# Decayed block attention feeding a SiLU MLP: transposes of q and k moved from TensorE to the DMA engines, and attention from block 8 on given due times

## The chip, the cores and the metric

One NeuronCore of a Trainium2 chip runs the whole program in one launch. The metric is device time in microseconds (us) of that core; lower is better. Times are medians over runs of the same kernel. One further execution was taken with the hardware profiler, and all durations below come from that execution.

## The reference

The input is q, k, v with 4 batches, 8 heads, 768 positions and 64 channels, a decay `lam` per head, and two weight matrices. The attention works on 64-position blocks with a running state per head:

```
intra = (qb @ kb.T * Dmask) @ vb            # Dmask[i,j] = lam**(i-j) for i >= j, else 0
inter = (qb * lam**(pos+1)) @ kv_state
out   = intra + inter
kv_state = lam**64 * kv_state + (kb * lam**(63-pos)).T @ vb
```

The attention result is laid out as x with 3072 rows (batch and position) and 512 columns (head and channel). Then comes the MLP: `h = x @ w_in` (512 to 2048), `g = h * sigmoid(h)`, `y = g @ w_out` (2048 to 512). The output is y, 3072 x 512 in float32.

## The kernel before

The kernel works on 24 blocks of 128 positions: block `u` belongs to batch `u // 6`, and the six blocks of a batch are chained through the state. Decay is folded into q and k: `qs` is q times a power of lam, `ks` is k times the inverse power, so the mask is only zeros and ones.

For each block the attention does this:

- SyncE (SP) issues the loads of k, v and q (`kf`, `vf`, `qf`). From block 2 to block 21, q comes for two blocks at once. All loads are issued in one fixed order from one queue, SP's, which also issues the output stores.
- VectorE makes `qs` (L315) and `ks` (L369) in bf16. For the first blocks (`u < WIDE`, WIDE = 8) `ks` is written into a zero-padded buffer instead (`kp`, L361), so that one transposed tile holds every head by itself.
- TensorE transposes `qs` (L327, four 128x128 matmuls per block) and `ks` (L389, four; with the padded form L377, eight) into a PSUM bank `tr_ps`. ScalarE, sometimes VectorE, copies the results out of PSUM (helper lines L224 and L226) to `qT` and to the zero-padded `kTz`.
- TensorE forms the scores `st_ps` (L415, eight matmuls), VectorE masks them into `st_sb` (L424), TensorE forms `x_ps` from the scores and from the state (L453, L457), and ScalarE copies that to `xt`, the transposed input of the MLP.
- TensorE forms the state's update `d_ps` (L484; in the padded form L480), VectorE adds it to the state (`y`, L500), and GpSimd scales by the decay (`Xz`, `Xf`, L229).

The MLP is done for groups of blocks. `first_product` (L545) multiplies `xt` of one group with `w_in`, ScalarE applies SiLU into `g` (L554), and `second_product` (L573; the last block L612) multiplies by `w_out`. VectorE copies the result out and SP stores it. A group of four blocks has matmuls with 512 moving columns, a group of two has 256, a group of one has 128.

The order of the work on every engine is fixed when the program is built. The class `Plan` holds every step with the cost that it books for it, its dependences, its ring buffers and a priority. It walks through time, always takes the step that can start first, and writes out the program in that order. The chip then runs each engine's list in order: an instruction that has to wait holds back everything behind it on its engine. `after` on a step adds booked time behind its dependences; a step on the engine `NONE` costs nothing and only delays what depends on it. Loads are written out 1.8 us ahead of the time at which they are booked (`AHEAD`). Where the plan leaves TensorE without work early on, `idle` fills the gap with matmuls on zeros (`warm_ps`, L650), of which it adds as many as fit:

```
us = 0.44 if a < 6 else 0.22
n = int(0.8 * (b - a - 0.2) / us)
if n < 2 or a > 90 or since > a: return
```

Of the kernel before, what the change touches and what calls it, by code (L numbers as in the profile page):

```python
# [8 lines left out]
BF16 = mybir.dt.bfloat16  # L9
# [4 lines left out]
class Plan:  # L14
# [3 lines left out]

    AHEAD = 1.8
    AWAY = 0.6  # L20
    LAT = {"SP": 0.0, "NONE": 0.0, "STORE": 2.0, "PE": 0.25, "DVE": 0.12, "ACT": 0.16, "POOL": 0.15, "DMA": 0.1}

    def __init__(self):
        self.ops = []
        self.rings = {}

    def op(self, engines, deps, fn, prio, alloc=(), frees=(), after=0.0):


        o = dict(engines=engines, deps=[d for d in deps if d is not None], fn=fn, prio=prio,  # L30
                 alloc=list(alloc), frees=list(frees), id=len(self.ops), end=None, slots={}, after=after)
        self.ops.append(o)
        return o

# [12 lines left out]
    def run(self, start, idle=None):  # L47
        INF = float("inf")
        free = dict(start)
        users = {}  # L50
        for o in self.ops:
            o["wait"] = len(o["deps"])
            for d in o["deps"]:
                users.setdefault(d["id"], []).append(o)
        ready = [o for o in self.ops if o["wait"] == 0]
        out = []
        while ready:
            pick = {}
            for o in ready:
                slots = max([self.slot(a)[1] for a in o["alloc"]] or [0.0])  # L60
                if slots == INF:
                    continue
                if "SP" in o["engines"]:
                    slots += self.AHEAD
                at = {e: max([free[e] if e != "NONE" else 0.0, slots] + [o["after"] + d["end"] + (self.LAT[d["eng"]] if d["eng"] != e else 0.0)
                                                 for d in o["deps"]]) for e in o["engines"]}
# [33 lines left out]
def kernel(  # L100
# [20 lines left out]
    KI = DM // 128  # L121
    KO = DFF // 128
    HB = BLK // 2
    WIDE = 8

    ctx.enter_context(tc.manual_schedule())
    const = ctx.enter_context(tc.tile_pool(name="const", bufs=1))
# [1 line left out]
    ps = ctx.enter_context(tc.tile_pool(name="ps", bufs=1, space=bass.MemoryType.PSUM))  # L129

    plan = Plan()
    BUFS = dict(kf=6, vf=6, qf=3, wst=6, qs=2, qT=4, ks=4, g=34, st_sb=6, o_sb=3, y=2, Xf=2,
                kTz=3, vz=3, Xz=2, kp=3)
    for name, n in BUFS.items():
        plan.ring(name, n)
    plan.ring("bank", 8, pick=True)
# [4 lines left out]
    def sb(o, name, shape, dtype, tag=None):  # L141
        return work.tile(shape, dtype, tag=tag or name, bufs=BUFS[tag or name], name=name)

    def bank(o, name, shape, dtype):
# [5 lines left out]
        out=lam_sb,  # L150
        in_=bass.AP(tensor=lam.tensor, offset=lam.offset, ap=[[0, 128]] + list(lam.ap)),
# [17 lines left out]
        out=ident, in_=ident, compare_op=AL.not_equal, fill=1.0,  # L169
# [6 lines left out]
        out=mask, in_=mask, compare_op=AL.is_ge, fill=0.0,  # L176
# [3 lines left out]
    kTz = [const.tile([128, NP, 2, BLK], BF16, name=f"kTz{i}") for i in range(BUFS["kTz"])]  # L180
# [22 lines left out]
    for hh in range(2):  # L203
        r = slice(64 * hh, 64 * hh + 64)
# [6 lines left out]
    w_in_r = moe_w_in.rearrange("(ko p) f -> p ko f", p=128)  # L211
    w_out_r = moe_w_out.rearrange("(ko p) f -> p ko f", p=128)

    groups = [[0, 1], [2, 3], [4], [5], [6, 7]] + [list(range(u, u + 4)) for u in range(8, NU, 4)]
    group_of = {u: (g, i) for g, us in enumerate(groups) for i, u in enumerate(us)}
    xts = [const.tile([128, KI, len(us) * BLK], BF16, name=f"xt{g}") for g, us in enumerate(groups)]

    plain = {0, 1, NU - 2, NU - 1}

    val = {}  # L220

    def copy(o, dst, src):
        if o["eng"] == "ACT":
            nc.scalar.activation(dst, src, AF.Copy)  # L224
        else:
            (nc.vector if o["eng"] == "DVE" else nc.gpsimd).tensor_copy(dst, src)  # L226
# [68 lines left out]
    O = {}  # L295

    def attention(u):
        b, blk = divmod(u, NB)
        pr = at["v", u]


        if u in plain or u % 2 == 0:
            two = u not in plain
            lq = load["q", u]
            late = []
            if u >= 8:
                late = [plan.op({"NONE": 0.0}, [lq], lambda o: None, 0, after=4.0)]
            halves = []
            for t in range(2 if two else 1):
                def fn(o, t=t, first=(t == 0)):  # L310
                    qf = val["qf", u]
                    if first:
                        val["qs", u] = sb(o, "qs", [128, 2, H, 64], BF16)
                    src = qf.rearrange("p h (t d) -> p h t d", t=2)[:, :, t, :] if two else qf
                    nc.vector.tensor_tensor(  # L315
                        val["qs", u][:, t], src,
                        lam_fwd[:, 1 + t if two else 0, :, None].to_broadcast([128, H, 64]), op=AL.mult)
                halves.append(plan.op(
                    {"DVE": 0.7}, [lq] + late + halves[:1], fn, pr + 0.1, alloc=["qs"] if t == 0 else [],
                    frees=[(lq, lq["tag"])] if t == two else []))  # L320
            trs = []
            for t in range(len(halves)):
                def fn(o, t=t):
                    if t == 0:
                        val["trq", u] = bank(o, "tr", [128, len(halves), NP, BLK], BF16)
                    for i in range(NP):
                        nc.tensor.transpose(val["trq", u][:, t, i, :], val["qs", u][:, t, 2 * i:2 * i + 2, :], ident)  # L327
                trs.append(plan.op({"PE": 0.225}, [halves[t]] + trs[:1], fn, pr + 0.1,
                                   alloc=["bank", "n_tr"] if t == 0 else [],
                                   frees=[(halves[0], "qs")] if t == len(halves) - 1 else []))  # L330
            evs = []
            for t in range(len(halves)):
                def fn(o, t=t):
                    if t == 0:
                        val["qT", u] = sb(o, "qT", [128, 2, NP, BLK], BF16)
                    copy(o, val["qT", u][:, t], val["trq", u][:, t])
                evs.append(plan.op({"ACT": 0.6, "DVE": 0.69}, [trs[t]] + evs[:1], fn, pr + 0.1,
                                   alloc=["qT"] if t == 0 else [],
                                   frees=[(trs[0], "bank"), (trs[0], "n_tr")] if t == len(halves) - 1 else []))
            O["qT", u] = evs  # L340
            if two:
                O["qT", u + 1] = evs
        home = u if u in plain else u - u % 2

        def qT(p):
# [5 lines left out]

        lk, lv = load["k", u], load["v", u]
        late = []
        if u >= 8:
            late = [plan.op({"NONE": 0.0}, [lv], lambda o: None, 0, after=4.0)]

        wide = u < WIDE
        if wide:
# [14 lines left out]
        if wide:  # L373
# [9 lines left out]
            kz = [plan.op({"ACT": 1.02, "DVE": 1.22}, [tk], fn, pr, alloc=["kTz"],  # L383
                          frees=[(tk, "bank"), (tk, "n_tr")])]
        else:
            def fn(o):
                val["trk", u] = bank(o, "tr", [128, NP, BLK], BF16)
# [135 lines left out]
        O["vz", u] = (vc, oo, dd)  # L523

    for u in range(NU):
        attention(u)
    for vc, oo, dd in (O["vz", u] for u in range(NU) if ("vz", u) in O):
        done = plan.op({"NONE": 0.0}, [oo, dd], lambda o: None, 0, frees=[(vc, "vz")])

# [120 lines left out]
                nc.tensor.matmul(t, lhsT=zeros[:, 0:128], rhs=zeros, start=True, stop=True)  # L650
        seq.append((a, len(seq), dict(fn=fn)))

    seq = plan.run({"PE": 1.9, "DVE": 4.2, "ACT": 5.9, "POOL": 5.0, "SP": 3.7, "STORE": 0.0, "NONE": 0.0}, idle)
    for _, _, o in seq:
        o["fn"](o)

# [29 lines left out]
```

## Time and profile before

| | us |
|---|---|
| median of 3 runs | 235.52 (235.09 to 236.05) |
| profiled execution, device time | 237.28 |
| its span in the profile | 235.6 |
| TensorE busy in the span | 221.8 |
| VectorE busy | 114.7 |
| ScalarE busy | 121.9 |
| GpSimd busy | 53.1 |

The profiled execution is 1.76 us above the median of the unprofiled runs, and 1.7 us of its device time lie outside the span. The span has three parts. Until about 30 us the first blocks' attention runs with little for TensorE to do beside it. From about 30 to 134 us attention and MLP matmuls are interleaved. From 134 us to the end only MLP matmuls are left. The granted TensorE clock was 0.998 of full speed over the span. TensorE's instructions are pipelined, so the time that one costs is the distance from its start to the next one's start, which is shorter than the duration that the group rows show for one.

### The profile page before, as it was taken

How to read it: one execution, taken by the hardware profiler on the slowest of the kernel's cores; microseconds unless marked ns; L12 is line 12 of the kernel's file. 1: busy time of each engine (PE TensorE's matmuls, PEld its weight loads, DVE VectorE, ACT ScalarE, POOL GpSimd, SP SyncE). 2: the span in 40 equal slices, each digit the busy share in tenths (PEclk: the TensorE clock that was granted, in tenths of full speed). 3: DMA queues.
4: the chain of work that ended last, by engine and by line, in shares of the span. 5: the costliest groups of instructions: out<-in, count | busy, mean ns of one | idle time of the engine just before them, and what ended most of it. 6: DMA issues, size and time to landing. Idle time of an engine off the chain costs nothing.

```text
span 235.6 us, 4440 instructions
## 1 busy us (share of the span) xinstructions
PE 221.8 (94%) x1799; PEld 136.3 (58%) x1799; DVE 114.7 (49%) x184; ACT 121.9 (52%) x213; POOL 53.1 (23%) x71
## 2 busy tenths in 40 slices
PE   4889898999999999979999999999999999999994
PEld 1656687899756676746667544444444444444453
DVE  5677755694359999998997211012100111021221
ACT  5585477867777699869976422401275023710000
POOL 7354420340045244642476100000000000000000
PEclk9999999999999999999999999999999999999999
DMA  6999989999999999999200122204400232023232
GB/s 124 237 288 298 294 227 226 296 363 318 221 228 245 255 262 222 233 238 219 46 1 12 35 47 45 45 2 87 92 0 0 45 75 61 0 45 83 56 86 89
DMA packets 73060, 33.85 MB, mean 144 GB/s; under 512 B 55376, under 2 KB 66000, under 8 KB 73040
## 3 DMA queue, kind: packets, MB, share of 16 engines
q1 hardware_dynamic: 72896, 33.50, 60.4%
q8 instruction: 14, 0.23, 0.4%
q10 hardware_dynamic: 144, 0.07, 0.1%
q14 instruction: 6, 0.05, 0.1%
HBM read 27.27 MB, written 6.29 MB: 142 GB/s over the span
## 4 chain that ended last, share of the span: by engine, by line
PE 52%; DVE 2%; DMA 1%; ACT 1%; issue 0%; DVEq 0%
PE o_ps L573 28%; PE h_ps L545 19%; PE x_ps L453 1%; PE st_ps L415 1%; DVE st_sb L424 1%; PE o_ps L612 1%; DMA out_dram<-o_sb 1%; PE x_ps L457 1%; PE d_ps L484 1%; PE tr_ps L327 0%; PE tr_ps L389 0%; DVE ks L369 0%; DVE y L500 0%; ACT kTz L224 0%; DVE o_sb L226 0%
## 5 line engine op out<-in xcount | busy, mean ns | idle before, releaser
L545 PE MATMUL h_ps<-xt,w_in_bf 128*128 128x512 bf16 (+2 forms) x576 | 88.9, 308 | 0.0
L554 ACT ACTIVATE g<-h_ps 128x512 bf16<-128x512 f32 x96 | 56.3, 597 | 59.2 <-PE h_ps L545 33.0
L573 PE MATMUL o_ps<-w_out_bf,g 128*128 128x512 bf16 x368 | 83.3, 379 | 0.5 <-DVE st_sb L424 0.5
L545 PEld LDWEIGHTS <-w_in_bf 128*128 128x128 bf16 x576 | 49.7, 98 | 29.1 <-DVE w_in_bf L226 0.3
L226 DVE COPY o_sb<-o_ps 128x512 f32<-128x512 f32 (+2 forms) x24 | 15.9, 663 | 87.1 <-PE o_ps L573 84.5
L573 PEld LDWEIGHTS <-g 128*128 128x128 bf16 x368 | 35.2, 98 | 39.6 <-issue 0.7
L229 POOL TENSOR_TENSOR Xz<-y,lam_blk 64x256 bf16<-64x256 f32 x40 | 34.3, 858 | 75.0 <-DVE y L500 46.0
L424 DVE TENSOR_TENSOR st_sb<-st_ps,mask 128x512 bf16<-128x512 f32 x48 | 30.9, 683 | 6.0 <-PE st_ps L415 5.7
L224 ACT ACTIVATE kTz<-tr_ps 64x512 bf16<-64x512 bf16 (+1 forms) x38 | 25.8, 680 | 6.6 <-PE tr_ps L377 2.2
L315 DVE TENSOR_TENSOR qs<-qf,lam_fwd 128x512 bf16<-128x512 f32 x24 | 20.2, 861 | 5.0 <-DMA qf<-in_q_dram 5.0
L224 ACT ACTIVATE xt<-x_ps 128x512 bf16<-128x512 f32 x24 | 14.2, 594 | 9.2 <-PE x_ps L457 8.8
L453 PE MATMUL x_ps<-st_sb,vz 128*128 128x128 bf16 x192 | 18.0, 219 | 0.2
L453 PEld LDWEIGHTS <-vz 128*128 128x128 bf16 x192 | 15.1, 98 | 5.4 <-issue 1.2
L500 DVE TENSOR_TENSOR y<-d_ps,Xf 64x256 f32<-64x256 f32 (+1 forms) x27 | 11.3, 419 | 9.9 <-issue 7.6
L415 PE MATMUL st_ps<-qT,kTz 128*128 128x128 bf16 x192 | 15.1, 222 | 0.5 <-ACT qT L224 0.3
L224 ACT ACTIVATE qT<-tr_ps 128x512 bf16<-128x512 bf16 x22 | 12.8, 594 | 4.4 <-PE tr_ps L327 4.3
L229 POOL TENSOR_TENSOR Xf<-y,lam_blk 128x256 f32<-128x256 f32 x16 | 14.5, 909 | 1.3
L457 PE MATMUL x_ps<-qT,Xz 128*128 128x128 bf16 x80 | 14.5, 219 | 0.0
L415 PEld LDWEIGHTS <-kTz 128*128 128x128 bf16 x192 | 12.5, 99 | 3.1 <-ACT kTz L224 1.0
L224 ACT ACTIVATE o_sb<-o_ps 128x512 f32<-128x512 f32 (+1 forms) x2 | 0.9, 438 | 25.6 <-DMA out_dram<-o_sb 25.6
L369 DVE TENSOR_TENSOR ks<-kf,lam_bwd 128x512 bf16<-128x512 f32 x16 | 14.0, 879 | 0.3
L327 PE MATMUL tr_ps<-ident,qs 128*128 128x128 bf16 x96 | 9.1, 223 | 4.0 <-DVE qs L315 3.8
(54 smaller groups left out, 115.8 us busy)
## 6 DMA issues: line engine op xcount, KB each, us to landing
kf<-in_k_dram SPq DMA_DIRECT2D x24, 256.0 KB, 5.5
vf<-in_v_dram SPq DMA_DIRECT2D x24, 256.0 KB, 5.3
out_dram<-o_sb SPq DMA_DIRECT2D x41, 128.0 KB, 2.4
qf<-in_q_dram SPq DMA_DIRECT2D x10, 512.0 KB, 5.9
wst<-in_moe_w_in_dram SPq DMA_DIRECT2D x8, 512.0 KB, 6.9
wst<-in_moe_w_out_dram SPq DMA_DIRECT2D x8, 512.0 KB, 7.3
qf<-in_q_dram SPq DMA_DIRECT2D x4, 256.0 KB, 5.1
out_dram<-o_sb SPq DMA_DIRECT2D x3, 256.0 KB, 3.6
```

Source lines behind the costliest of these rows:

```text
L224: nc.scalar.activation(dst, src, AF.Copy)
L226: (nc.vector if o["eng"] == "DVE" else nc.gpsimd).tensor_copy(dst, src)
L229: (nc.vector if o["eng"] == "DVE" else nc.gpsimd).tensor_tensor(dst, a, b, op=op)
L315: nc.vector.tensor_tensor(val["qs", u][:, t], src, lam_fwd[:, 1 + t if two else 0, :, None].to_broadcast([128, H, 64]), op=AL.mult)
L369: nc.vector.tensor_tensor(val["ks", u], val["kf", u], lam_bwd[:, :, None].to_broadcast([128, H, 64]), op=AL.mult)
L415: nc.tensor.matmul(val["st", u, half][:, i, :], lhsT=val["kTz", u][:, h // 2, h % 2, :], rhs=qT(h // 2), start=True, stop=True)
L424: nc.vector.tensor_tensor(val["st_sb", u, half], val["st", u, half], m[:, None, :].to_broadcast([128, 4, BLK]), op=AL.mult)
L453: nc.tensor.matmul(x[:, p, :], lhsT=vp[:, p, hh, :], rhs=val["st_sb", u, h // 4][:, h % 4, :], start=(hh == 0), stop=(hh == 1 and blk == 0))
L457: nc.tensor.matmul(x[:, p, :], lhsT=val["Xz", u][:, p, :], rhs=qT(p), start=False, stop=True)
L545: nc.tensor.matmul(t[:, j, :], lhsT=w_in_bf[:, ko, (m * per + j) * 128:(m * per + j + 1) * 128], rhs=xts[g][:, ko, :], start=(ko == 0), st ...
L554: nc.scalar.activation(t, val["h", g, m], AF.Silu)
L573: nc.tensor.matmul(val["o", u], lhsT=val["g", g, ko][:, i * BLK:(i + 1) * BLK], rhs=w_out_bf[:, ko, :], start=(ko == 0), stop=(ko == KO - 1))
```

## The change

- From block 8 on (`XB = 8`) the transposes of `qs` and `ks` are DMA transposes, issued by SP from SBUF to SBUF. The q transpose of a pair of blocks is one DMA of 128 x 1024 bf16, that of a single block and each k transpose one of 128 x 512. The k transposes land in a new ring `kT` (3 buffers), and ScalarE or VectorE copies them from there to `kTz`. `qT` is written by the DMA itself.
- The plan knows these DMAs as an engine of their own, `XBAR`, with 2.0 us booked per 512 columns. What reads the result is booked no earlier than 6.0 us after that.
- Attention steps from block 8 on get due times: `pace(u)` is 57.0 + 5.5 (u - 8) us. Their q, k and v are used no earlier than that, and no earlier than 2.0 us after the load's booked end (4.0 before). For blocks 4 to 7 that delay is 1.2 us (none before). TensorE steps of the attention from block 8 on get `after = 0.8`.
- `WIDE` goes from 8 to 4, so that blocks 4 to 7 use the unpadded form. The ring `qf` has 2 buffers in place of 3.
- Blocks 8 to 11 form two groups of two in place of one group of four.

```diff
+    XB = 8
-    WIDE = 8
+    WIDE = 4
-    BUFS = dict(kf=6, vf=6, qf=3, ...
+    BUFS = dict(kf=6, vf=6, qf=2, ... kT=3)
-    groups = [[0, 1], [2, 3], [4], [5], [6, 7]] + [list(range(u, u + 4)) for u in range(8, NU, 4)]
+    groups = [[0, 1], [2, 3], [4], [5], [6, 7], [8, 9], [10, 11]] + [list(range(u, u + 4)) for u in range(12, NU, 4)]
+    def pace(u):
+        return 0.0 if u < 8 else 57.0 + 5.5 * (u - 8)
...
-            if u >= 8:
-                late = [plan.op({"NONE": 0.0}, [lq], lambda o: None, 0, after=4.0)]
+            if u >= 4:
+                late = [plan.op({"NONE": 0.0}, [lq], lambda o: None, 0, after=2.0 if u >= 8 else 1.2, at=pace(u))]
...
+            if u >= XB:
+                n = len(halves)
+                def fn(o):
+                    val["qT", u] = sb(o, "qT", [128, 2, NP, BLK], BF16)
+                    nc.sync.dma_start_transpose(
+                        out=val["qT", u][:, 0:n].rearrange("p t a s -> p (t a) s"),
+                        in_=val["qs", u][:, 0:n].rearrange("p t h d -> p (t h d)"))
+                x = plan.op({"XBAR": 2.0 * n}, [halves[-1]], fn, pr + 0.1, alloc=["qT"], frees=[(halves[0], "qs")])
+                O["qT", u] = [x, plan.op({"NONE": 0.0}, [x], lambda o: None, 0, after=6.0)]
...
+        elif u >= XB:
+            def fn(o):
+                val["kT", u] = sb(o, "kT", [128, NP, BLK], BF16)
+                nc.sync.dma_start_transpose(
+                    out=val["kT", u], in_=val["ks", u].rearrange("p h d -> p (h d)"))
+            tk = plan.op({"XBAR": 2.0}, [ks], fn, pr, alloc=["kT"])
+            landed = plan.op({"NONE": 0.0}, [tk], lambda o: None, 0, after=6.0)
+            ...
+                    copy(o, val["kTz", u][r, :, hh, :], val["kT", u][r])
+                kz.append(plan.op({"ACT": 0.59, "DVE": 0.35}, [tk, landed] + kz[:1], fn, pr, ...
...
     for u in range(NU):
+        n = len(plan.ops)
         attention(u)
+        if u >= 8:
+            for o in plan.ops[n:]:
+                if "PE" in o["engines"]:
+                    o["after"] = 0.8
```

More of the change, by code (lines that the diff above doesn't have):

```diff
@@ L20 @@
     AWAY = 0.6
-    LAT = {"SP": 0.0, "NONE": 0.0, "STORE": 2.0, "PE": 0.25, "DVE": 0.12, "ACT": 0.16, "POOL": 0.15, "DMA": 0.1}
+    LAT = {"SP": 0.0, "XBAR": 0.0, "NONE": 0.0, "STORE": 2.0, "PE": 0.25, "DVE": 0.12, "ACT": 0.16, "POOL": 0.15, "DMA": 0.1}
     def __init__(self):
@@ L25, in __init__, with op @@
         self.rings = {}
-    def op(self, engines, deps, fn, prio, alloc=(), frees=(), after=0.0):
+    def op(self, engines, deps, fn, prio, alloc=(), frees=(), after=0.0, at=0.0):
         o = dict(engines=engines, deps=[d for d in deps if d is not None], fn=fn, prio=prio,
-                 alloc=list(alloc), frees=list(frees), id=len(self.ops), end=None, slots={}, after=after)
+                 alloc=list(alloc), frees=list(frees), id=len(self.ops), end=None, slots={}, after=after, at=at)
         self.ops.append(o)
@@ L64, in run @@
                     slots += self.AHEAD
-                at = {e: max([free[e] if e != "NONE" else 0.0, slots] + [o["after"] + d["end"] + (self.LAT[d["eng"]] if d["eng"] != e else 0.0)
+                at = {e: max([free[e] if e != "NONE" else 0.0, slots, o["at"]] + [o["after"] + d["end"] + (self.LAT[d["eng"]] if d["eng"] != e else 0.0)
                                                  for d in o["deps"]]) for e in o["engines"]}
@@ L131 @@
     plan = Plan()
-    BUFS = dict(kf=6, vf=6, qf=3, wst=6, qs=2, qT=4, ks=4, g=34, st_sb=6, o_sb=3, y=2, Xf=2,
-                kTz=3, vz=3, Xz=2, kp=3)
+    BUFS = dict(kf=6, vf=6, qf=2, wst=6, qs=2, qT=4, ks=4, g=34, st_sb=6, o_sb=3, y=2, Xf=2,
+                kTz=3, vz=3, Xz=2, kp=3, kT=3)
     for name, n in BUFS.items():
@@ L321, in attention @@
             trs = []
-            for t in range(len(halves)):
+            if u >= XB:
[7 more added lines that the diff above has]
+                O["qT", u] = [x, plan.op({"NONE": 0.0}, [x], lambda o: None, 0, after=6.0)]
+            for t in range(len(halves) if u < XB else 0):
                 def fn(o, t=t):
@@ L331, in attention @@
             evs = []
-            for t in range(len(halves)):
+            for t in range(len(halves) if u < XB else 0):
                 def fn(o, t=t):
@@ L339, in attention @@
                                    frees=[(trs[0], "bank"), (trs[0], "n_tr")] if t == len(halves) - 1 else []))
-            O["qT", u] = evs
+            if u < XB:
+                O["qT", u] = evs
             if two:
-                O["qT", u + 1] = evs
+                O["qT", u + 1] = O["qT", u]
         home = u if u in plain else u - u % 2
@@ L353, in attention @@
         late = []
-        if u >= 8:
-            late = [plan.op({"NONE": 0.0}, [lv], lambda o: None, 0, after=4.0)]
+        if u >= 4:
+            late = [plan.op({"NONE": 0.0}, [lv], lambda o: None, 0, after=2.0 if u >= 8 else 1.2, at=pace(u))]
         wide = u < WIDE
@@ L384, in attention, with fn @@
                           frees=[(tk, "bank"), (tk, "n_tr")])]
+        elif u >= XB:
[5 more added lines that the diff above has]
+            landed = plan.op({"NONE": 0.0}, [tk], lambda o: None, 0, after=6.0)
+            kz = []
+            for hh in range(2):
+                def fn(o, hh=hh):
+                    if hh == 0:
+                        val["kTz", u] = kTz[o["slots"]["kTz"]]
+                    r = slice(64 * hh, 64 * hh + 64)
+                    copy(o, val["kTz", u][r, :, hh, :], val["kT", u][r])
+                kz.append(plan.op({"ACT": 0.59, "DVE": 0.35}, [tk, landed] + kz[:1], fn, pr,
+                                  alloc=["kTz"] if hh == 0 else [], frees=[(tk, "kT")] if hh else []))
         else:
@@ L651, in idle @@
         seq.append((a, len(seq), dict(fn=fn)))
-    seq = plan.run({"PE": 1.9, "DVE": 4.2, "ACT": 5.9, "POOL": 5.0, "SP": 3.7, "STORE": 0.0, "NONE": 0.0}, idle)
+    seq = plan.run({"PE": 1.9, "DVE": 4.2, "ACT": 5.9, "POOL": 5.0, "SP": 3.7, "STORE": 0.0, "NONE": 0.0, "XBAR": 0.0}, idle)
     for _, _, o in seq:
```

## The prediction

> **What bounds the kernel now.** I read the page first, then busy time by stretch, then the chain of waits, then TensorE's and VectorE's instructions in order of time, and last the DMA queue of the loading stretch.
>
> From the page:
>
> ```profile
> span 235.6 us, 4440 instructions
> ...
> PE 221.8 (94%) x1799; PEld 136.3 (58%) x1799; DVE 114.7 (49%) x184; ACT 121.9 (52%) x213; POOL 53.1 (23%) x71
> ...
> PE   4889898999999999979999999999999999999994
> ...
> DVE  5677755694359999998997211012100111021221
> ...
> DMA  6999989999999999999200122204400232023232
> ```
>
> A slice is 5.9 us. TensorE is full from slice 8 to the end but for one dip at about 103 us. VectorE is full only in slices 13 to 21 (71 to 124 us), and the DMA engines are full until slice 19 and nearly idle after it. By stretch (busy us of PE, PEld, DVE, ACT, POOL; clock; DMA share; GB/s):
>
> ```profile
> 30.00:60.00 30.00, 28.24 (x398) 26.42 (x396) 19.91 (x32) 22.26 (x36) 6.51 (x8) 1.00 1.04 283
> 60.00:110.00 50.00, 48.23 (x478) 32.88 (x476) 42.61 (x67) 40.15 (x73) 20.29 (x22) 1.00 1.08 238
> 110.00:130.00 20.00, 19.54 (x201) 13.33 (x200) 16.78 (x29) 15.95 (x30) 11.19 (x14) 1.00 0.23 42
> 130.00:236.00 106.00, 102.25 (x505) 48.30 (x503) 14.46 (x22) 25.70 (x45) 0.18 (x1) 0.99 0.22 49
> ```
>
> From 30 to 130 us TensorE idles 1.76 + 1.77 + 0.46 = 4.0 us; everything else is matmuls back to back. So a matmul that goes away shortens the kernel by its whole cost, as long as nothing new makes TensorE wait. From 134 us on there are MLP products alone, which the change does not touch. The chain that ended last (start, us, what) gives the cost of one matmul in the queue:
>
> ```profile
> 103.45 0.40 PE d_ps L484 x4
> 103.84 0.22 PE tr_ps L389 x4
> 104.07 1.73 PE h_ps L545 x8
> ...
> 106.91 0.45 PE tr_ps L327 x8
> ```
>
> A 128-column transpose costs 0.45/8 = 0.056 us, a 512-column product 1.73/8 = 0.216. TensorE's own order adds two forms:
>
> ```profile
> 22.20 0.40 PE L480 MATMUL d_ps<-vz,kp 128*128 128x64 bf16 x8
> 22.44 1.04 PE L545 MATMUL h_ps<-xt,w_in_bf 128*128 128x256 bf16 x8
> ...
> 59.73 3.77 PE L545 MATMUL h_ps<-xt,w_in_bf 128*128 128x256 bf16 x33
> 63.33 0.39 PE L327 MATMUL tr_ps<-ident,qs 128*128 128x128 bf16 x4
> ```
>
> Thirty-three 256-column products take 63.33 - 59.73 = 3.60 us, 0.109 each; eight padded state updates take 0.24 us, no more than the four unpadded ones.
>
> **Part 1, transposes leave TensorE.** From block 8 on, 16 blocks have 4 k and 4 q transposes each: 128 matmuls. With WIDE = 4, blocks 4 to 7 need 4 k transposes in place of 8: 16 more. 144 x 0.056 = 8.1 us, all in stretches where TensorE is full: **-8.1**. The state updates of blocks 4, 6 and 7 cost the same in both forms (0.24 against 0.22): nothing.
>
> One skill page rates a TensorE transpose far higher. "VectorE: DVE Perf Modes", section "The three transpose paths", gives 390 ns for 128x128 and 1309 ns for the DMA path, and its rules say to use TensorE if a PSUM destination is acceptable, which speaks against this change. By 390 ns the 144 would be worth 56 us; the chain's 56 ns per transpose contradicts that, and I use the chain.
>
> **Part 2, two groups of two.** Group 8 to 11 had 64 products of 512 columns, 64 x 0.216 = 13.8 us; now 128 of 256 columns, 128 x 0.109 = 13.95: **+0.1**. The SiLU work keeps its tile size.
>
> **Part 3, due times.** In the new program's order there are 29 warm-up matmuls in place of 27; the two new ones stand ahead of the products of blocks 6 and 7. The planner's formula adds exactly two only for a gap of 0.75 to 1.02 us, so it leaves TensorE without work there, where it had work before: **+0.9** (0.4 if only the two matmuls of 0.216 count, 1.0 at most).
>
> Against that, the same due times thin out VectorE. Its worst stall of TensorE now reads:
>
> ```profile
> 100.71 1.21 DVE L315 TENSOR_TENSOR qs<-qf,lam_fwd 128x512 bf16<-128x512 f32 x1
> 101.84 1.21 DVE L369 TENSOR_TENSOR ks<-kf,lam_bwd 128x512 bf16<-128x512 f32 x1
> 102.98 0.41 DVE L226 CAST vz<-vf 128x512 bf16<-128x512 f32 x1
> ```
>
> The state update at 103.45 us waited 1.39 us for that `vz`, behind a `qs` and a `ks` that took 1.21 us each. The work that VectorE now does in about 60 us (70 to 130) is spread to about 145, since block 23 is due at 57 + 5.5 x 15 = 139.5. Blocks 4 to 7 also get 1.2 us of lateness. Between nothing and all of the 4.0 us of idle goes; I take half: **-2.0**. What is late next is the transposed tile.
>
> **Part 4, the DMA transposes.** There are 25 of them: 16 for k and 2 for q of 128 KB, 7 for q pairs of 256 KB, so 32 units of 128 KB, 4.2 MB. No DMA transpose is in the trace. Two things can hurt.
>
> First, room on the DMA engines, full until about 114 us (the share of 0.23 in the 20 us from 110 on is 4.6 us):
>
> ```profile
> DMA packets 37204, 11.91 MB, mean 238 GB/s; under 512 B 30543, under 2 KB 36687, under 8 KB 37199
> ...
> kf<-in_k_dram SPq DMA_DIRECT2D x14, 256.0 KB, 5.4
> ```
>
> That is the loading stretch, 60 to 110 us. At its 238 GB/s a unit takes 0.55 us, and 32 take 18 us; at the fastest slice (363 GB/s) 0.36. The upper bound is 2.4 us, the landing time of a whole 128 KB store, which would be 77 us. More traffic can't speed the loads, so there is no gain. I take 0.55, from the row that it is nearest to: transfers into SBUF in the same queue, 30543 of whose 37204 packets are under 512 bytes. Then loading ends near 114 + 18 = 132 us, before block 23 is due: no cost, because the due times are the cover.
>
> A second skill page agrees in size: "DMA: Bandwidth & Descriptors", section "Latency and other measured facts", has 261 GB/s for DMA transposes with a non-contiguous middle dimension, an estimate of 0.5 us per unit. By the 1309 ns of the other page a unit would be 5.2 us, an estimate of 168 us for all 32, far beyond any cover. The two pages contradict each other, and no run here shows either.
>
> Second, SP's queue. A transpose waits there for `ks` or `qs`, a q transpose also for a free `qT`, and the next blocks' loads and output stores stand behind it. Loads land 5.4 us after issue in the full stretch, small stores 2.4 us in the median of the whole run, so some 3 us of SP waiting are covered by transfers still queued. The cover of the result is 8 us (2.0 booked plus 6.0) for a k transpose and 10 for a pair of q, against 5.4 for a load of twice the k transpose's size. Behind a late result stand `kTz` on ScalarE with the SiLUs behind it, then the scores on TensorE with all products behind them. TensorE catches up nothing, so the largest lateness counts once. I take **+1.5**, between 0 (inside the cover) and 5 (one queue's depth of 5.4).
>
> The vanished PSUM copies (14 of `qT` at 0.59 us on ScalarE) lie beside TensorE: nothing by themselves. The `kTz` copies stay, 28 on ScalarE and 4 on VectorE.
>
> **Sum.** -8.1 + 0.1 + 0.9 - 2.0 + 1.5 = -7.6. The profiled 237.28 would become 229.7, with a span near 228.0; the median 235.52 lies 1.76 lower, so 227.9 us. With all bounds at their best -8.1 + 0.1 + 0.4 - 4.0 = -11.6 (223.9), at their worst -8.1 + 0.1 + 1.0 + 5 = -2.0 (233.5).
>
> **Rivals.**
>
> *The transposes fill the DMA engines (slower).* For: the DMA share is 1.08 from 60 to 110 us, and the transposes come on top. Place: TensorE waits at the scores, ever longer from about 90 us on. Lateness starts where 114 + 32c passes 145 us, the end of block 23's due slot: c = 0.97 us per unit. It outweighs the 7.6 us at c = 1.2. At c = 1.5, lateness is 114 + 48 - 145 = 17, net +9.4: about 245 us. Against: in bytes the transposes are a third of the loads from block 8 on (12.6 MB), and those move at 0.55 us per 128 KB.
>
> *The waits return through SP (small gain).* Each transpose is cheap on the engines but lands 3 to 7 us past its cover, since SP holds it behind stores and loads that wait for buffers (`qf` has only 2). TensorE loses that once or twice: 231 to 235 us. Against: 8 and 10 us of cover.
>
> *The transposes were free filler (no change).* If TensorE took them while it waited for VectorE anyway, removing them shows idle instead: 235.5. Against: only 4.0 us of idle in 100 us, so at most half could hide so.
>
> **How the numbers follow.** The main case 0.70, waits through SP 0.09, filler 0.03, full DMA engines 0.18. The range 224.5 to 238.0 holds nearly all of the first three cases and the lower edge of the last, about 0.8. A measurement of this kernel can tell about 0.5% (1.2 us) from no change. Faster by more: 0.70 plus most of the second, 0.75. Same: 0.05. Slower: the last case and a little of the second, 0.20.
>
> **What would show it.** Right: about 80 transposes left on TensorE (224 before); TensorE idle from 30 to 130 us under 5 us; VectorE near 7 tenths from 60 to 145 us; transposes landing within 8 us; loads ending near 130; only products after about 150. Wrong: gaps on TensorE ended by `kTz` or `qT` that grow with time, landings of the transposes above 10 us, or SP waiting long at the new kernel's L332 and L404 while the DMA share is low.

## The result and the profile after

| | before | after |
|---|---|---|
| median, us (lowest to highest) | 235.38 (235.09 to 236.05), 4 runs | 232.08 (231.64 to 233.37), 4 runs |
| profiled execution, us | 237.28 | 231.64 |
| its span | 235.6 | 229.9 |
| TensorE busy / idle in the span | 221.8 / 13.8 | 215.3 / 14.6 |

The ratio of after to before is 0.9865 (95% interval 0.982 to 0.991), a gain of 3.3 us. The forecast was 227.9, a gain of 7.6. The direction held and the time lies in the range, but more than half of the expected gain is missing. The time is that of the rival "The waits return through SP", 231 to 235 us. Some executions of a kernel took over 1.5% longer than its fastest, mostly at a lower granted clock; they are left out of the medians below, and the profiles of e5, e6 and e8, which are of such executions, are not read.

The page of the kernel after, with the rows that answer to those shown of before:

```profile
span 229.9 us, 4320 instructions
...
PE 215.3 (94%) x1709; PEld 135.2 (59%) x1709; DVE 114.2 (50%) x191; ACT 111.8 (49%) x197; POOL 49.8 (22%) x71
...
PE   4989999999999897769999999999999999999994
...
DVE  5686767686448781656687575862110210021221
...
DMA  5999999999999999999999992430040242024232
```

TensorE is busy 6.5 us less, as the transposes left. But its row now has a hole in slices 14 to 18, about 75 to 103 us, where before only slice 18 dipped. VectorE is no longer full from slice 13 to 21. The DMA row is full for five slices more. By stretch (length, busy us of PE, PEld, DVE, ACT and POOL, granted clock, DMA share, GB/s), the kernel after:

```profile
30.00:60.00 30.00, 29.75 (x392) 27.66 (x391) 21.06 (x36) 24.19 (x44) 6.14 (x8) 1.00 1.06 285
60.00:110.00 50.00, 43.55 (x367) 29.87 (x366) 29.35 (x49) 24.15 (x43) 13.62 (x17) 1.00 1.14 224
110.00:130.00 20.00, 20.00 (x161) 11.74 (x159) 13.86 (x23) 9.66 (x18) 6.77 (x9) 1.00 1.15 212
130.00:236.00 106.00, 96.57 (x562) 48.98 (x559) 29.09 (x49) 35.47 (x63) 8.55 (x11) 1.00 0.28 62
```

From 30 to 60 and from 110 to 130 us TensorE has no idle time to speak of. From 60 to 110 us it idles 50.00 - 43.55 = 6.45 us, against 1.77 before. TensorE's instructions in that stretch name what ended the gaps (start, duration, form, count, idle time before it and its releaser):

```profile
88.18 0.23 PE L447 MATMUL st_ps<-qT,kTz 128*128 128x128 bf16 x1 [1.25 <-ACT kTz L229]
...
102.69 0.23 PE L447 MATMUL st_ps<-qT,kTz 128*128 128x128 bf16 x1 [1.55 <-ACT kTz L229]
```

They are scores that wait for `kTz`, the zero-padded copy of the transposed k tile. The chain of waits in the same stretch follows one of them back (start, us, what):

```profile
82.56 0.58 SPq L266
...
83.25 4.17 DMA kT<-ks
...
87.49 0.64 ACT kTz L229
88.15 0.64 ACT kTz L229
...
88.83 0.34 PE st_ps L447 x3
```

A load's issue on SP, then the k transpose behind it (4.17 us from its issue to its landing), then two copies to `kTz`, then the scores: the new kernel's path between 80 and 105 us is mostly this, and `DMA kT<-ks` has 46% of it. The landing is not long. What is late is the issue, as block 13 shows (VectorE makes `ks`, then SP issues its transpose):

```profile
84.86 0.69 DVE L385 TENSOR_TENSOR ks<-kf,lam_bwd 128x512 bf16<-128x512 f32 x1
...
98.13 1.62 SPq L404 DMA_TRANSPOSE kT<-ks  x1
```

`ks` was done at 85.55 us and its transpose was issued 12.6 us later; for blocks 11 and 12 it was 10.2 and 10.1. The experiments ask why.

### The profile page after: what moved, and what is told of

Same layout as the page of the kernel before. It is cut to its first block, busy times and chain, and to the rows that moved or that the text cites. A ratio compares the mean times of both kernels' runs of the same rounds, so it can differ in the third digit from the quotient of the medians.

```text
span 229.9 us, 4320 instructions
## 1 busy us (share of the span) xinstructions
PE 215.3 (94%) x1709; PEld 135.2 (59%) x1709; DVE 114.2 (50%) x191; ACT 111.8 (49%) x197; POOL 49.8 (22%) x71
## 4 chain that ended last, share of the span: by engine, by line
PE 71%; DMA 14%; SPq 8%; ACT 2%; DVE 2%; issue 1%; DVEq 0%; ACTq 0%
PE h_ps L583 31%; PE o_ps L611 29%; DMA kT<-ks 7%; SPq L266 5%; DMA wst<-in_moe_w_in_dram 4%; PE st_ps L447 3%; PE x_ps L485 3%; DMA kf<-in_k_dram 2%; ACT kTz L229 2%; PE x_ps L489 1%; PE d_ps L516 1%; SPq L274 1%; DVE st_sb L456 1%; PE o_ps L650 1%; DMA out_dram<-o_sb 1%
## 5 line engine op out<-in xcount | busy, mean ns | idle before, releaser
L583 PE MATMUL h_ps<-xt,w_in_bf 128*128 128x256 bf16 (+2 forms) x640 | 90.7, 294 | 0.3 <-ACT xt L229 0.3
L583 PEld LDWEIGHTS <-w_in_bf 128*128 128x128 bf16 x640 | 55.9, 98 | 22.8 <-PE warm_ps L688 0.6
L234 POOL TENSOR_TENSOR Xz<-y,lam_blk 64x256 bf16<-64x256 f32 x40 | 32.6, 815 | 102.4 <-DVE y L532 36.7
L456 DVE TENSOR_TENSOR st_sb<-st_ps,mask 128x512 bf16<-128x512 f32 x48 | 32.3, 688 | 19.2 <-PE st_ps L447 18.9
L229 ACT ACTIVATE kTz<-kT 64x512 bf16<-64x512 bf16 x28 | 17.6, 628 | 23.2 <-DMA kT<-ks 22.8
L447 PE MATMUL st_ps<-qT,kTz 128*128 128x128 bf16 x192 | 18.2, 223 | 5.3 <-ACT kTz L229 4.5
L447 PEld LDWEIGHTS <-kTz 128*128 128x128 bf16 x192 | 13.7, 99 | 12.9 <-ACT kTz L229 6.4
L320 DVE TENSOR_TENSOR qs<-qf,lam_fwd 128x512 bf16<-128x512 f32 x24 | 18.5, 794 | 3.8 <-DMA qf<-in_q_dram 3.7
L229 ACT ACTIVATE vz<-vf 128x512 bf16<-128x512 f32 x14 | 8.8, 630 | 10.6 <-DMA vf<-in_v_dram 10.4
L234 POOL TENSOR_TENSOR Xf<-y,lam_blk 128x256 f32<-128x256 f32 x16 | 12.9, 808 | 1.3
L688 PE MATMUL warm_ps<-zeros 128*128 128x512 bf16 x29 | 9.5, 448 | 1.3 <-DVE pos L162 1.3
```

The lines of the kernel that those rows point to most:

```text
L234: (nc.vector if o["eng"] == "DVE" else nc.gpsimd).tensor_tensor(dst, a, b, op=op)
L320: nc.vector.tensor_tensor(val["qs", u][:, t], src, lam_fwd[:, 1 + t if two else 0, :, None].to_broadcast([128, H, 64]), op=AL.mult)
L447: nc.tensor.matmul(val["st", u, half][:, i, :], lhsT=val["kTz", u][:, h // 2, h % 2, :], rhs=qT(h // 2), start=True, stop=True)
L456: nc.vector.tensor_tensor(val["st_sb", u, half], val["st", u, half], m[:, None, :].to_broadcast([128, 4, BLK]), op=AL.mult)
L583: nc.tensor.matmul(t[:, j, :], lhsT=w_in_bf[:, ko, (m * per + j) * 128:(m * per + j + 1) * 128], rhs=xts[g][:, ko, :], start=(ko == 0), st ...
```

## The experiments

Medians are in us with lowest and highest; each ratio is against the kernel before on the same chip. The runs are from several chips, on which the kernel before took 235.38 to 235.84, so differences between two medians are good to about half a microsecond.

**How much of the idle time was real.** The kernel before, unchanged.

> The kernel before, unchanged, profiled once more. Its first profiled execution took 237.28 us while its unprofiled runs had a median of 235.4. If TensorE's 4.0 us of idle between 30 and 130 us belong to the kernel, the new profile shows 3.5 to 4.5 us again and a span near 235.6. If part of them was an accident of that one execution, the new profile shows about 2 us of idle there and a span near 233.7, and the saving that the prediction made of them was never to be had in the median.

Measured: 235.8 (235.14 to 236.28, 10 runs), ratio 1.0003 (0.998 to 1.0026). Its profiled execution took 235.37 us, not 237.28. The stretches of this run:

```profile
30.00:60.00 30.00, 29.63 (x409) 27.70 (x408) 19.67 (x32) 23.34 (x39) 6.56 (x8) 1.00 1.05 288
60.00:110.00 50.00, 48.23 (x474) 32.22 (x472) 42.90 (x67) 40.47 (x74) 20.26 (x22) 1.00 1.08 239
```

The idle time from 30 to 60 us is 0.37, where the first profile had 1.76. The 1.77 us from 60 to 110 are there again. So the 4.0 us of idle of the prediction were 2.6 in this execution, which is near the median, and 1.4 of them belonged to the one execution that was profiled first.

**The early part alone.** The kernel before with

```diff
-    WIDE = 8
+    WIDE = 4
-            if u >= 8:
-                late = [plan.op({"NONE": 0.0}, [lq], lambda o: None, 0, after=4.0)]
+            if u >= 4:
+                late = [plan.op({"NONE": 0.0}, [lq], lambda o: None, 0, after=4.0 if u >= 8 else 1.2)]
```

and the same for k and v.

> The kernel before with only the early part of the change: unpadded form from block 4 on and 1.2 us of lateness for blocks 4 to 7. The transposes stay on TensorE, no due times. Theory: the early part is worth about 3 us by itself, since the change cut TensorE's idle before 60 us from 8.2 to 4.8 us; idle before 60 us under 5.5 us, median 232 to 233. Rival: what is gained early is lost again where VectorE is full (70 to 124 us), since TensorE only arrives earlier at the same waits; idle from 60 to 130 us then rises above 4 us and the median stays at 234.5 or more.

Measured: 237.41 (235.88 to 238.5, 10 runs), ratio 1.0061 (1.0028 to 1.0094), 0.6% slower. Taking 16 transposes off blocks 4 to 7 and making these blocks later gained nothing without the rest. TensorE idles 3.8 us from 60 to 110, and one stretch and one instruction show how:

```profile
100.00:110.00 10.00, 7.55 (x60) 5.20 (x59) 8.39 (x14) 5.69 (x11) 3.27 (x4) 0.83 0.97 220
```

```profile
105.98 0.27 PE L453 MATMUL x_ps<-st_sb,vz 128*128 128x128 bf16 x2 [2.35 <-DVE st_sb L424]
```

TensorE waited 2.35 us for VectorE, which was busy for 8.39 of these 10 us, and the granted clock of the stretch was 0.83. The loss goes with the clock: the two of the ten executions with a mean granted clock of 1.00 took 235.88 and 235.93, no longer than the kernel before, and the eight slower ones had 0.985 to 0.993.

**Due times without DMA transposes.** The kernel after with all transposes on TensorE.

```diff
-    XB = 8
+    XB = 24
```

> The changed kernel with all transposes on TensorE again (XB = 24), everything else as changed: due times, lateness, groups. Theory (the DMA transposes make the transposed tiles late): TensorE's 6.5 us of idle from 60 to 110 us fall under 2 us, TensorE gets 128 x 0.056 = 7.2 us of transposes back, together about +2: median 233 to 235. Rival (the due times and the new order make TensorE wait, whoever transposes): idle from 60 to 110 us stays near 6 us and the median is 238 to 240.

Measured: 231.48 (231.21 to 231.74), ratio 0.9819 (0.9789 to 0.985).

```profile
60.00:110.00 50.00, 49.77 (x494) 36.76 (x492) 35.90 (x58) 36.58 (x67) 18.66 (x22) 1.00 0.96 210
```

This is 4.1 us below the kernel before and not slower than the whole change. From 60 to 110 us TensorE idles 0.23 us. Compared with it, the kernel after has 220.87 - 215.31 = 5.6 us less work on TensorE and 14.6 - 8.7 = 5.9 us more idle time. The 128 transposes were taken away, and about as much time came back as waiting.

To see whether the two groups of two matter, the same kernel with blocks 8 to 11 in one group of four:

```diff
-    groups = [[0, 1], [2, 3], [4], [5], [6, 7], [8, 9], [10, 11]] + [list(range(u, u + 4)) for u in range(12, NU, 4)]
+    groups = [[0, 1], [2, 3], [4], [5], [6, 7]] + [list(range(u, u + 4)) for u in range(8, NU, 4)]
```

> The changed kernel with all transposes on TensorE and blocks 8 to 11 in one group of four again, due times as changed. The kernel with TensorE transposes and two groups of two took 231.5. Theory (the due times bring the gain, the groups cost 0.1): median 231 to 232, TensorE's idle from 60 to 130 us under 1 us. Rival (with due times the attention comes later, and without the two small groups TensorE has too little to do between 60 and 100 us): idle of 2 us or more there, or more warm-up matmuls, median 233 to 236.

Measured: 231.85 (231.59 to 232.45), ratio 0.9855 (0.9828 to 0.9883). The groups are worth 0.4 us at most, and the ranges overlap. So the gain of 4.1 us comes from the due times with what goes along with them: the unpadded form and the lateness of blocks 4 to 7, the 2.0 us behind a load, the 0.8 us on TensorE's steps and the smaller ring `qf`. Of these only the part of blocks 4 to 7 was run alone (e1), without gain; the due times alone were not.

**Is it the cover?** If k transposes are merely later than booked, using them later must help. First the kernel after with later due times:

```diff
-        return 0.0 if u < 8 else 57.0 + 5.5 * (u - 8)
+        return 0.0 if u < 8 else 66.0 + 5.5 * (u - 8)
```

> The changed kernel with one number changed: due times start at 66 us in place of 57, at the same 5.5 us per block. Theory (loads and transposes together fill the DMA engines, and the due times of blocks 9 to 16 come before their tiles can have landed): with 9 us more the tiles are in time, idle from 60 to 110 us falls from 6.5 to under 2 us, median 226 to 228. Rival (SP's queue holds the transposes back behind waits that move along with the due times): transposes start later by as much, idle stays above 4 us, median 230 to 233.

Measured: 227.5 (227.01 to 227.97), ratio 0.9651 (0.9617 to 0.9684).

```profile
60.00:110.00 50.00, 48.63 (x382) 31.82 (x380) 32.39 (x52) 21.21 (x39) 11.99 (x14) 1.00 1.07 217
```

The idle time from 60 to 110 us falls from 6.45 to 1.37 and the kernel gains 4.6 us. Then the same due times with the transposes on TensorE, so that the later times and the DMA transposes can be told apart:

```diff
-    XB = 8
+    XB = 24
-        return 0.0 if u < 8 else 57.0 + 5.5 * (u - 8)
+        return 0.0 if u < 8 else 66.0 + 5.5 * (u - 8)
```

> The changed kernel with all transposes on TensorE and due times from 66 us: what the DMA transposes are worth where they are in time. Theory: TensorE idles no less than with due times from 57 us (0.2 us from 60 to 110 us there), so the median stays at 231 to 232.5, and the DMA transposes with the same due times (227.5) are worth 4 to 5 us of the 7.2 us of TensorE time that they remove. Rival (the later due times alone bring the gain of the kernel with due times from 66 us): median 228 to 229.

Measured: 230.95 (230.65 to 231.64), ratio 0.9814 (0.9785 to 0.9843). Later due times bring 0.5 us with TensorE's transposes and 4.6 with DMA transposes, so they act through the DMA transposes. At these due times the DMA transposes are worth 230.95 - 227.5 = 3.45 us. Last, the kernel after with its own due times and more booked cover, at both places:

```diff
-                O["qT", u] = [x, plan.op({"NONE": 0.0}, [x], lambda o: None, 0, after=6.0)]
+                O["qT", u] = [x, plan.op({"NONE": 0.0}, [x], lambda o: None, 0, after=12.0)]
-            landed = plan.op({"NONE": 0.0}, [tk], lambda o: None, 0, after=6.0)
+            landed = plan.op({"NONE": 0.0}, [tk], lambda o: None, 0, after=12.0)
```

> The changed kernel with due times from 57 us as they are, and the booked time from a transpose's end to the use of its result raised from 6.0 to 12.0 us. Theory: what failed is the cover, since the k tiles of blocks 9 to 16 landed up to 8.2 us after the booked use; 6 us more cover takes most of that, idle from 60 to 110 us under 2.5 us, median 227 to 229, close to the kernel with due times from 66 us. Rival: only later loads' use helps, since lateness grows with every block until the DMA engines catch up; idle moves to after 110 us and the median stays above 230.

Measured: 228.43 (227.48 to 229.16), ratio 0.9702 (0.966 to 0.9744). Two unlike ways to use the tiles later both come within 0.6 us of the forecast's time. Too little cover is shown as the place of the loss.

**Why the tiles are late: room on the DMA engines, or SP's queue?** Each DMA transpose of the kernel after split into two halves of the columns. The bytes stay, the instructions double from 25 to 50.

```diff
-                nc.sync.dma_start_transpose(
-                    out=val["kT", u], in_=val["ks", u].rearrange("p h d -> p (h d)"))
+                ki = val["ks", u].rearrange("p h d -> p (h d)")
+                for c in range(2):
+                    nc.sync.dma_start_transpose(
+                        out=val["kT", u][:, 2 * c:2 * c + 2], in_=ki[:, c * 256:(c + 1) * 256])
```

The q transposes are split alike.

> The changed kernel with each DMA transpose split into two of half the columns: 50 instructions on SP in place of 25, the same bytes. Theory D (the DMA engines have no room: a 128 KB unit costs 0.7 to 0.9 us of them, and everything behind comes that much later): bytes are the same, so idle from 60 to 110 us stays at 6 to 8 us and the median at 231.5 to 233.5. Rival S (SP's queue is the limit: each transpose holds it 1.2 to 3.1 us): 25 further holds of at least 1.2 us are 30 us more on SP; idle from 60 to 110 us well above 10 us, median 240 or more.

Measured: 246.85 (245.78 to 248.49), ratio 1.0491 (1.0436 to 1.0546). The k transposes on SP's queue (lowest, median and highest hold in ns; first and last start), whole in the kernel after and then halved:

```profile
L404 SPq DMA_TRANSPOSE kT<-ks x16: 1188/1483/2834, 66.2 to 147.4; - x16
...
DMA to landing us min/median/max: 2.4/3.7/5.5
```

```profile
L409 SPq DMA_TRANSPOSE kT<-ks x32: 1168/1242/2720, 66.5 to 167.6; - x32
```

A half holds SP's queue about as long as a whole: 1.17 against 1.19 us at least. The q pairs, twice as large, take 1.22. The 25 added instructions are 25 x 1.24 = 31 us of SP's queue. The stretch of this run shows that it was not the DMA engines that limited it:

```profile
60.00:110.00 50.00, 38.44 (x314) 25.45 (x311) 27.20 (x45) 18.36 (x33) 12.27 (x14) 1.00 0.94 195
```

TensorE idles 11.6 us while the DMA share falls from 1.14 to 0.94. To take the transposes' own engine work out of the question, the kernel after with two DMAs of 512 bytes behind each transpose, whose result nobody reads:

```diff
+    tiny = [const.tile([16, H], F32, name=f"tiny{i}") for i in range(12)]
+    used = [0]
+    def issue_tiny():
+        for _ in range(2):
+            nc.sync.dma_start(
+                out=tiny[used[0] % 12],
+                in_=bass.AP(tensor=lam.tensor, offset=lam.offset, ap=[[0, 16]] + list(lam.ap)))
+            used[0] += 1
...
                     out=val["kT", u], in_=val["ks", u].rearrange("p h d -> p (h d)"))
+                issue_tiny()
```

> The changed kernel with two tiny DMAs (16 x 8 float32, 512 bytes, read by nothing) issued on SP behind each DMA transpose: 50 instructions more on SP, 25 KB more on the DMA engines. Theory S (SP's queue is the limit: in the changed kernel its DMA instructions take 73.6 us of the stretch from 58 to 138 us): 50 x 0.4 to 0.5 = 20 to 25 us more on SP, the last load lands at 150 us or later in place of 136, idle from 60 to 110 us above 10 us, median 240 to 250. Theory D (the DMA engines are the limit): next to no bytes, the last load stays within 2 us of 136, median 231 to 234.

Measured: 244.96 (243.79 to 245.45), ratio 1.0384 (1.0345 to 1.0422).

```profile
60.00:110.00 50.00, 39.61 (x316) 26.41 (x318) 26.96 (x43) 19.90 (x36) 12.28 (x14) 0.96 0.94 193
```

Fifty DMAs with 26 KB among them hold SP's queue 0.565 us each in the median, 28 us in all, and the kernel loses 12.9. The DMA share falls to 0.94 again. A microsecond added on SP's queue costs nearly half a microsecond of the kernel. Not all of it is waiting: TensorE's busy time is 218.7 us here and 218.9 in e4, against 215.3, at a mean granted clock of 0.979 and 0.986.

The next test adds bytes as well as instructions: each k transpose is issued a second time, into a spare buffer.

```diff
+                nc.sync.dma_start_transpose(
+                    out=sb(o, "kS", [128, NP, BLK], BF16), in_=val["ks", u].rearrange("p h d -> p (h d)"))
                 nc.sync.dma_start_transpose(
                     out=val["kT", u], in_=val["ks", u].rearrange("p h d -> p (h d)"))
```

> The changed kernel with each k transpose issued twice, the second time into a spare buffer that nothing reads: 16 units of 128 KB more on the DMA engines and 16 instructions more on SP. Theory D: by 130 us the loads come 16 x 0.7 to 0.9 = 11 to 14 us later than in the changed kernel, and TensorE waits for most of it; median 239 to 246. Rival S predicts about as much, by 16 holds of 1.2 us or more. Third possibility (the transposes' cost is their latency after issue, neither room nor queue): a copy behind the needed one delays little, median under 235. Together with the split kernel: under D this one is far slower than the split one, under S the split one is at least as slow.

Measured: 243.68 and 246.0, ratio 1.04 (1.0331 to 1.0468). The 16 added instructions cost about 12.8 us, 0.80 each, where e4's 25 without new bytes cost 0.59 each. So bytes may cost something too, but this run changes both.

Then relief. The v loads from block 8 on leave SP's queue, first for GpSimd's, then for ScalarE's:

```diff
-                nc.sync.dma_start(out=t, in_=src[b, :, sl, :].rearrange("h s d -> s h d"))
+                (nc.gpsimd if kind == "v" and j >= 8 else nc.sync).dma_start(out=t, in_=src[b, :, sl, :].rearrange("h s d -> s h d"))
```

> The changed kernel with the loads of v from block 8 on issued by GpSimd in place of SP: 16 loads fewer on SP's queue, the same bytes on the same DMA engines. Theory D (no room on the DMA engines): idle from 60 to 110 us stays at 5 to 8 us, median 231 to 234. Rival S (SP's queue is the limit): SP is free for about 16 us more, transposes start earlier, idle falls under 3 us, median 227 to 229.

Measured: 230.41 to 238.0. Three of its four executions are left out as said above, and nothing is concluded from the one at 230.41. With `nc.scalar` in that place:

> The changed kernel with the loads of v from block 8 on issued from ScalarE's queue in place of SP's: 16 loads of 0.5 to 1.9 us of issue time leave SP, the bytes stay. Theory D: idle from 60 to 110 us stays at 5 to 8 us and the last load still lands near 136 us; median 231 to 234. Rival S: transposes are issued earlier, idle under 3 us, median 227 to 229.

Measured: 230.4 (229.83 to 231.22), ratio 0.9793 (0.976 to 0.9825).

```profile
60.00:110.00 50.00, 44.96 (x374) 30.63 (x377) 30.20 (x51) 24.03 (x43) 15.24 (x17) 1.00 1.22 227
```

Sixteen loads fewer on SP bring 1.7 us, not the whole loss. TensorE still idles 5.0 us here. The DMA share rises to 1.22, the k transposes now land 5.2 us after issue in the median, 3.7 before, and each holds SP 2.16 us in the median, 1.48 before. So SP gained less than the 16 loads had taken. This reads as DMA engines without room, which holds up the issue too.

So traffic was cut as well. First alone: the kernel after with q pairs from block 8 on loaded only by half, both halves of the pair computed from the first. This leaves part of q out of the computation.

```diff
+                if j >= 8:
+                    nc.sync.dma_start(
+                        out=t[:, :, 0:64],
+                        in_=q[b, :, blk * BLK:(blk + 2) * BLK, :].rearrange("h (p t) d -> p h t d", t=2)[:, :, 0, :])
...
-                    src = qf.rearrange("p h (t d) -> p h t d", t=2)[:, :, t, :] if two else qf
+                    src = qf.rearrange("p h (t d) -> p h t d", t=2)[:, :, 0 if u >= 8 else t, :] if two else qf
```

> The changed kernel with half of each q pair's load left out from block 8 on (256 KB in place of 512; both halves of the pair use the loaded one, so this leaves out part of the q data): 1.8 MB less on the DMA engines, the same number of instructions on SP. Theory D (no room on the DMA engines): loads come 14 x 0.55 = 7.7 us earlier by the end and about 4 us earlier where TensorE waits, idle from 60 to 110 us falls from 6.5 to 1 to 3 us, median 227.5 to 229.5. Rival S (SP's queue is the limit at 25 transposes too): the holds stay, idle stays at 5 to 7 us, median 231 to 233.

Measured: 229.56 (228.4 to 230.0), ratio 0.9744 (0.9703 to 0.9786), a gain of 2.5 us. With the same number of instructions on SP, fewer bytes alone help, as the theory of full DMA engines had it. And both reliefs together, with part of q left out likewise:

> The changed kernel with both reliefs: half of each q pair's load left out from block 8 on (part of the q data is left out) and the v loads issued from ScalarE's queue. Each alone let the last load land at 134.2 and 133.3 us in place of 136.1 and left 6.0 and 5.0 us of idle from 60 to 110 us. If SP's queue and the DMA engines limit close behind each other, both together bring more than the sum: last load before 129 us, idle under 3 us, median under 229. If one of them alone is the limit, it brings what that one brought: last load near 133 us, median 229.5 to 231.

Measured: 227.39 (226.28 to 228.19), ratio 0.9642 (0.9601 to 0.9684).

```profile
60.00:110.00 50.00, 47.71 (x406) 32.78 (x409) 32.80 (x55) 25.29 (x45) 15.12 (x17) 1.00 1.25 214
```

Together they bring 4.7 us, about the sum of 1.7 and 2.5 apart, and most of the 5.9 that came back as waiting. So there are two limits close together, SP's queue and the DMA engines; which of them comes first is not shown. The last load lands at 126.9 us here, at 136.1 in the kernel after and at 114.1 before.

**A version that beats both.** Later due times and the v loads on ScalarE's queue:

```diff
-                nc.sync.dma_start(out=t, in_=src[b, :, sl, :].rearrange("h s d -> s h d"))
+                (nc.scalar if kind == "v" and j >= 8 else nc.sync).dma_start(out=t, in_=src[b, :, sl, :].rearrange("h s d -> s h d"))
-        return 0.0 if u < 8 else 57.0 + 5.5 * (u - 8)
+        return 0.0 if u < 8 else 66.0 + 5.5 * (u - 8)
```

> The kernel with due times from 66 us (227.5 us) with its v loads from block 8 on issued from ScalarE's queue: the candidate for the best version. It has 1.4 us of idle from 60 to 110 us left. Theory S: transposes land earlier, that idle falls under 0.6 us, median 226.3 to 227.0. Rival: with the due times late enough SP has slack, and the loads on ScalarE's queue only delay its copies: median 227.3 to 228.5.

Measured: 226.52 (225.69 to 227.13), ratio 0.9597 (0.9558 to 0.9635), the fastest of all. It computes everything. Over e3 it gains 1.0 us, with ranges that touch. Where that comes from is not shown: its profiled execution took 227.13, as long as e3's, and idles no less from 60 to 110 us (1.83 us against 1.37), where the expectation had under 0.6.

## Why the prediction was wrong in its size

**Failed: the term "+1.5" for waits on the DMA transposes, bounded by 5.** Measured against e2, which is the same kernel without them, the waits cost 5.9 us of idle time: more than the upper bound, and as much as the work saved. In the prediction's own terms, the 128 transposes gave -5.6 of busy time where -7.2 stood, the rest of parts 1 to 3 gave -4.1 (e2) where -1.9 stood, and the waits +5.9 where +1.5 stood. That makes -3.8, near the 3.7 us between the profiled executions of e0 and the kernel after. Two sentences of part 4 were wrong.

The first is "Then loading ends near 114 + 18 = 132 us, before block 23 is due: no cost, because the due times are the cover." The end of loading was nearly right (136.1 measured), but it was held against the last block alone. Set against the landings that the plan books, block 23's k transpose was 1.1 us late, those of blocks 11 to 20 were 4.3 to 8.6 us late. Block 13's landed at 101.98 us, booked 93.8. TensorE's gaps stand where the lateness grows: at 76, 88, 94 and 103 us, with blocks 9, 11, 12 and 13, late by 1.2, 4.3, 5.3 and 8.2 us. The later blocks up to 20 are late by 4.4 to 8.6, and from 110 to 130 us TensorE has no gap. So the prediction's rule that the largest lateness counts once roughly fits; its bound for that lateness, one queue's depth of 5.4 us, was too small. A cover has to be checked for each block.

The second is that "some 3 us of SP waiting are covered by transfers still queued". The prediction took SP's queue as a place of waits only and gave a DMA transpose no time of its own there. Each one holds the queue 1.2 us or more, 25 of them some 30 us at least, where a load takes 0.6. SP's rows of the kernel after have no pause while blocks 12 and 13 wait (start, us, what):

```profile
88.85 0.59 SPq L266 DMA_DIRECT2D vf<-in_v_dram  x1
89.55 1.33 SPq L404 DMA_TRANSPOSE kT<-ks  x1
90.98 0.53 SPq L269 DMA_DIRECT2D qf<-in_q_dram  x1
91.60 2.37 SPq L332 DMA_TRANSPOSE qT<-qs  x1
94.06 1.18 SPq L635 DMA_DIRECT2D out_dram<-o_sb  x2
```

In the kernel before, the same queue:

```profile
92.71 0.95 SPq L261 DMA_DIRECT2D vf<-in_v_dram  x1
93.71 1.93 SPq L261 DMA_DIRECT2D kf<-in_k_dram  x1
95.73 1.01 SPq L261 DMA_DIRECT2D vf<-in_v_dram  x1
96.78 1.01 SPq L264 DMA_DIRECT2D qf<-in_q_dram  x1
```

There a load holds SP 1 us or more (medians from 58 to 140 us: 1.42 for k, 1.06 for v). After, it holds SP about 0.6 (0.58 and 0.64). This reads as a backlog of transfers behind SP before, and little of it after, so that less was left to cover SP's time; no run tests that by itself. Of these two views the first was in reach before the prediction: back-to-back issues on SP in the loading stretch say that an added instruction on SP is not free. That the wider hold is 1.2 us could not be seen, but a bound of 25 x 1 us from the loads' own rows would have shown the danger.

**The rival that came had the place right, and its mechanism in part.** "SP holds it behind stores and loads", and a landing "3 to 7 us past its cover" (up to 8.6 measured), is what the rows and e4 and e12 show. That these "wait for buffers" is not shown: the rows have SP issuing one transfer after another. It was given a chance of 0.09 because "8 and 10 us of cover" was counted from the booked issue, not from the real one. The landing itself was as forecast: 3.7 us in the median for k and 3.3 for q, 5.8 at most, all under 8.

**The rival of full DMA engines** did not come with its size, about 245 us. The DMA share rose only to 1.14, and it fell where the kernel lost most (e4, e12). But it had a part in the loss: fewer bytes alone gained 2.5 us (e8). The estimate of 0.55 us per unit gave an end of loading at 132 us, 4 us early.

**Part 1 was near as a price.** About 5.6 us of TensorE's busy time went with the 128 transposes, and 6.7 between e7 and e3; 128 x 0.056 = 7.2 was expected. That the 16 early ones would be worth 0.9 us by themselves is not seen in e1, which is no faster: there TensorE idles 3.8 us from 60 to 110 us in place of 1.8, 3.3 of it in two waits for VectorE's `st_sb`.

**Parts 2 and 3 were too low together.** The working gives -0.9 for the 16 early transposes, +0.1, +0.9 and -2.0, so -1.9, and e2 measured -4.1. The +0.9 was right, though little of it shows as idle time, since the two new warm-up matmuls fill it. In the kernel after:

```profile
51.94 0.59 PE L688 MATMUL warm_ps<-zeros 128*128 128x512 bf16 x2
52.79 1.47 PE L583 MATMUL h_ps<-xt,w_in_bf 128*128 128x256 bf16 x12 [0.25 <-ACT xt L229]
```

From the one start to the other are 0.85 us, and as much in e2. The idle time from 30 to 130 us fell by 2.1 in e2 against e0 (2.6 to 0.5). Of the rest, 0.6 us lie before 30 us, and 1.4 are less busy time, of which the early transposes would be 0.9. The -2.0 was half of a sum in which 1.4 us were an accident of the profiled execution; of the 2.6 that e0 has, the due times and what goes with them took nearly all. VectorE's share from 60 to 110 us fell from 0.85 to 0.59, somewhat below the 0.7 forecast.

**The two pages of the Trainium skill.** The 1309 ns per 128x128 of "VectorE: DVE Perf Modes", section "The three transpose paths", would make an estimate of 5.2 us for a 128x512 DMA transpose. It does not add up that way: one lands 2.4 us after its issue at the least, 3.7 in the median. The 56 ns of a TensorE transpose in the stream stand against its 390 ns. That page's advice to stay on TensorE holds for the change as made, e2 being no slower, but not with more cover (e7 against e3), and in neither case for the reason of its figures. The 261 GB/s of "DMA: Bandwidth & Descriptors", section "Latency and other measured facts", can't be judged here: no run takes the DMA engines' time for a transpose by itself.

**Still open.** Why a DMA transpose holds the queue 1.2 us whatever its size, and how much of the waiting on SP is this hold, how much the wait of a DMA for the completion of earlier ones, was not separated. Nor was it shown which of the two limits, SP's queue or the DMA engines, comes first, nor was it tried to issue the transposes themselves from another queue.

## What to carry to other kernels

When work moves from a full engine to DMAs, cost the issuing queue like an engine: so many instructions by the hold of each, next to what it already issues back to back in that stretch. Check the cover of a moved step block by block, from the time at which it can really be issued, not at the last block. And profile the kernel before twice before its idle time goes into a sum.

## What the runs showed of the hardware

- A DMA transpose of bf16 held SP's queue at least 1.17 us for 128x256, 1.19 for 128x512 and 1.22 for 128x1024. A load of 256 KB held it 0.37 us at the least, and a DMA of 512 bytes 0.565 in the median. A few wide DMA transposes were much cheaper here than many narrow ones: with each split in two, the kernel lost 14.8 us.
- Copies to `kTz` from SBUF in place of PSUM took 290 ns on VectorE (413 before) and 627 on ScalarE (588 before).
- In e1 the granted TensorE clock was 0.83 over 100 to 110 us, after waits of 0.91 us (until 97.97) and 2.35 us (until 105.98); from 107 to 110 us it was 0.50. It was 1.00 in the same stretch of e0.
